# Measured VectorE durations in a kernel's own static schedule, and weight loads three groups later

## The chip, the cores and the metric

The kernel runs on one core of one Trainium2 chip. The metric is the device time of one execution in microseconds (us). Before the change the median was 1032.4 us (three runs, 1031.57 to 1032.62). The profile is one further execution of 1032.84 us, whose span from first to last instruction was 1031.0 us.

## The reference, cut to what matters

Linear attention produces 4608 tokens of width 512. A gate gives each token a score for each of eight experts, eight rounds of row and column normalisation turn the scores into a table P, and the output is the sum of eight two-layer experts, each weighted by its column of P.

```
x = attention(q, k, v, w_phi)            # 8 x 8 heads, 576 tokens, width 64 -> [4608, 512]
P = np.exp(x @ w_gate - max)             # [4608, 8]
for _ in range(8):                       # the "routing"
    P /= P.sum(1, keepdims=True) + 1e-09
    P /= P.sum(0, keepdims=True) + 1e-09
    P *= N / E
for e in range(8):
    out += P[:, e:e+1] * (np.maximum(x @ w1[e], 0) @ w2[e])
```

## The kernel before

The kernel orders its own instructions. Each operation is first recorded with an engine and an estimated duration; a list scheduler in the kernel then plays the whole program through with those estimates and so fixes one order per engine. On the chip every engine works through its list in order and waits where data is not there yet (in the routing's timeline below, a small matmul that waits 0.47 us holds up the large ones behind it). So a wrong estimate never breaks the result, but it places an operation too early or too late among its neighbours.

```
class Op:
    def after(self, user):                       # when a user of this operation may start
        if user.eng == self.eng and not self.nbytes:
            return self.stop + (0.0 if self.eng == "PE" else 0.04)
        return self.end
# ... cut ...
def dve(el, fn, r=(), w=(), shared=False):       # VectorE: el is an estimate in elements
    plan.op("DVE", el / 960.0 + 0.07, 0.15, fn, r, w, shared=shared)
```

The routing is a chain on VectorE. Each of its eight rounds ends in one small matmul (24 columns) that sums over partitions. Meanwhile TensorE has the matmuls of expert 0, so the small matmuls are put between those.

```
for it in range(8):
    # u = L * c_bc; rr = 1 / sum(u); wv = L * rr; cs = column sum of wv; two subtractions
    pe(24, ... mm(pc, colw, high(cs)) ...)       # the small matmul
    # c_bc = 1 / sum of the three parts in pc
```

Experts 1 to 7 each take nine groups of 512 tokens. They use sums of quarter matrices so that seven products do the work of eight. In expert 1 the sums of x ("X sums") are made by VectorE in buffers S, stored to DRAM, and read back by every expert as X. The sums of an expert's weights are made by VectorE from the freshly loaded w1 and w2.

```
ring("s_p", [128, 4, 256], BF16, "S", 5)         # five buffers S: X sums and hidden sums
# ... cut ...
for e in range(1, E):
    w1, w2 = load_w(e, ["late", ("acc", 2, 0, 0)] if e > 1 else ["late"])
    # ... cut: sums of weights, groups
```

The key `("acc", 2, 0, 0)` makes the load wait for the last write to that accumulator, which is group two of the preceding expert.

## Time and profile before

| stage (profile of before) | from, to (us) | TensorE |
|---|---|---|
| attention, with expert 0 begun | 0 to 204 | some 11 us idle, 10 of them in the first 60 us |
| routing beside expert 0 | 204 to 253 | small waits at seven small matmuls |
| experts 1 to 7 | 253 to 1020 | one gap, at 310 us, otherwise nearly full |
| last products and store | 1020 to 1031 | 4.5 us idle at the end |

The first lines are from the page: busy time and share of the span of each engine, and the chain of waits that ended last.

```profile
PE 1010.8 (98%) x9469; PEld 838.2 (81%) x9504; DVE 826.1 (80%) x1600; ACT 705.9 (68%) x1530; POOL 458.3 (44%) x480
...
PE 90%; DVE 4%; ACT 3%; DMA 2%; issue 1%; SPq 0%; DVEq 0%; ACTq 0%
```

TensorE (PE) bounds the kernel, so only its idle time can be won. The next lines are its timeline in the routing of the kernel before. The columns are the start, the length, engine, line, operation, output and inputs, sizes and number; in brackets stands the idle time before it and what ended it. Of the names, cs holds the column sums, hT the hidden values of an expert, and ps is an accumulator of TensorE.

```profile
211.15 1.89 PE L573 MATMUL ps<-xT,w 128*128 128x512 bf16 x8
213.35 0.17 PE L573 MATMUL ps<-cs,colw 128*128 128x24 bf16 x1 [0.31 <-DVE cs L1129]
213.37 1.89 PE L573 MATMUL ps<-w,hT 128*128 128x512 bf16 x8
...
217.03 0.17 PE L573 MATMUL ps<-cs,colw 128*128 128x24 bf16 x1 [0.47 <-DVE cs L1129]
```

The small matmul at 213.35 us waits for VectorE's last subtraction, and the eight large ones behind it wait too. The bracket understates the loss: ends of matmuls are modelled, and the eight before it were issued at 0.2155 us each, so the next could have started at 212.87 us. Seven small matmuls wait like this. The same chain on VectorE, one round of it, in the timeline of before:

```profile
221.61 0.20 DVE L1138 RECIPROCAL c_bc<-c_bc 128x8 f32<-128x8 f32 x1
221.84 0.46 DVE L1111 TENSOR_TENSOR T<-L,c_bc 128x288 f32<-128x288 f32 x1
222.34 0.45 DVE L1114 TENSOR_REDUCE rr<-T 128x36 f32<-128x288 f32 x1
222.82 0.38 DVE L1116 RECIPROCAL rr<-rr 128x36 f32<-128x36 f32 x1
223.24 0.46 DVE L1117 TENSOR_TENSOR T<-L,rr 128x288 f32<-128x288 f32 x1
223.73 0.68 DVE L1120 TENSOR_REDUCE cs<-T 128x8 f32<-128x288 f32 x1
224.44 0.37 DVE L1129 TENSOR_TENSOR cs<-cs 128x8 f32<-128x8 f32 x2
225.09 0.18 DVE L1135 TENSOR_REDUCE c_bc<-ps 128x8 f32<-128x24 f32 x1 [0.28 <-PE ps L573]
```

VectorE has no rest in the chain except for the matmul. The plan's estimate for the 288-element operations was 0.37 us; from the multiply at 221.84 to the reduce that needs it are 0.50 us.

The second place is expert 1, where expert 2's weights are loaded at 296.57 us. The chain of waits of before in this window (start, length, what):

```profile
298.14 8.75 DMA xd<-S
306.88 0.02 issue
306.91 2.43 DVE S L1181 x3
309.34 0.61 DVE hT L1305
309.95 0.04 issue
310.00 2.02 PE ps L1273 x17
```

A store of X sums takes 8.75 us, VectorE waits for the buffer that it reads, and TensorE waits for VectorE. The matmul before the gap was issued at about 308.55 us; at 0.109 us each the next was due at 308.66, so 1.34 us are lost.

### The profile page before, as it was taken

To read this page: it belongs to the slowest core of one execution; us is meant where nothing else is said; L and a number is where in the kernel's file an instruction comes from. 1 tells how busy PE (TensorE), PEld (TensorE's weight loads), DVE (VectorE), ACT (ScalarE), POOL (GpSimd) and SP (SyncE) were. 2 spreads that over 40 slices of the span, in tenths; PEclk is the share of its full clock that TensorE was granted. 3 is DMA by queue.
4 is the path that set the end of the run, shared out by engine and by line. 5 is a ranking of instruction groups with operands and counts; after the bars stand their busy time and mean duration, and the time that the engine had idled before them with its cause. 6 is when DMAs were issued, how large, how long until landed. Compare 5 with 4: busy or idle time off the path is not lost.

```text
span 1031.0 us, 24290 instructions
## 1 busy us (share of the span) xinstructions
PE 1010.8 (98%) x9469; PEld 838.2 (81%) x9504; DVE 826.1 (80%) x1600; ACT 705.9 (68%) x1530; POOL 458.3 (44%) x480
## 2 busy tenths in 40 slices
PE   7899999999999999999999999999999999999998
PEld 5666666635888888888888888888888888888886
DVE  7999989985889877778787877787787778777775
ACT  7999999834877766666665666666666666666663
POOL 5778764400344444444444434444444443344342
PEclk9999999999999999999999999999999999999999
DMA  9999977160263212511161116111431116114333
GB/s 254 178 192 190 179 131 124 35 150 1 97 139 114 63 42 57 108 42 52 43 129 47 42 43 123 42 52 37 85 88 50 42 43 123 42 42 126 131 124 123
DMA packets 112500, 96.03 MB, mean 93 GB/s; under 512 B 54144, under 2 KB 87040, under 8 KB 112384
## 3 DMA queue, kind: packets, MB, share of 16 engines
q1 hardware_dynamic: 80576, 70.55, 26.5%
q0 software_dynamic: 31648, 23.86, 16.3%
q8 instruction: 74, 1.21, 0.5%
q14 instruction: 42, 0.34, 0.1%
q10 hardware_dynamic: 160, 0.07, 0.0%
HBM read 94.98 MB, written 14.16 MB: 106 GB/s over the span
## 4 chain that ended last, share of the span: by engine, by line
PE 90%; DVE 4%; ACT 3%; DMA 2%; issue 1%; SPq 0%; DVEq 0%; ACTq 0%
PE ps L1273 72%; PE ps L573 15%; PE ps L856 2%; DMA xd<-S 1%; ACT q L569 1%; ACT k L569 1%; DMA acc<-in_k_dram 1%; DVE S L1181 0%; PE ps L703 0%; DVE cs L1120 0%; DVE m L565 0%; DVE wx L565 0%; DVE T L1111 0%; DVE T L1117 0%; DVE rr L1114 0%
## 5 line engine op out<-in xcount | busy, mean ns | idle before, releaser
L1428 POOL TENSOR_TENSOR acc<-acc,V 128x512 f32<-128x512 f32 x248 | 314.5, 1279 | 490.1 <-ACT V L1425 428.6
L1301 ACT COPY U<-ps 128x512 f32<-128x512 f32 x378 | 216.9, 587 | 169.9 <-PE ps L1273 157.5
L1305 DVE CUSTOM_DVE_ANT_0 hT<-ps,U 128x512 bf16<-128x512 f32 x378 | 254.3, 686 | 83.1 <-PE ps L1273 56.3
L1425 ACT ACTIVATE V<-ps,P 128x256 f32<-128x256 f32 x496 | 208.7, 475 | 88.1 <-PE ps L1273 81.4
L1413 DVE SCALAR_TENSOR_TENSOR acc<-ps,P,acc 128x256 f32<-128x256 f32 x372 | 158.6, 476 | 72.1 <-PE ps L1273 72.0
L1273 PEld LDWEIGHTS <-S 128*128 128x128 bf16 x1984 | 194.1, 98 | 22.6
L1273 PEld LDWEIGHTS <-T 128*128 128x128 bf16 x1512 | 147.9, 98 | 17.4 <-issue 0.3
L1273 PEld LDWEIGHTS <-hT 128*128 128x128 bf16 x1488 | 145.6, 98 | 16.9
L1273 PE MATMUL ps<-X,T 128*128 128x256 bf16 x1008 | 150.2, 273 | 0.0
L1273 PE MATMUL ps<-T,S 128*128 128x256 bf16 x1056 | 135.8, 273 | 0.0
L1273 PEld LDWEIGHTS <-wx 128*128 128x128 bf16 x1152 | 112.7, 98 | 14.9 <-issue 1.6
L1181 DVE TENSOR_TENSOR S<-hT 128x1024 bf16<-128x1024 bf16 x124 | 91.3, 742 | 9.9 <-ACT hT L1310 9.9
L1273 PEld LDWEIGHTS <-w 128*128 128x128 bf16 x864 | 84.5, 98 | 9.8
L1273 PE MATMUL ps<-xT,wx 128*128 128x256 bf16 x576 | 88.5, 273 | 1.2 <-DVE hT L1305 1.2
L1273 PE MATMUL ps<-X,wx 128*128 128x256 bf16 x576 | 86.8, 273 | 0.0
L1310 ACT ACTIVATE hT<-ps 128x512 bf16<-128x512 f32 x126 | 72.9, 608 | 7.8 <-PE ps L1273 7.8
L1273 PE MATMUL ps<-wx,hT 128*128 128x256 bf16 x560 | 77.3, 273 | 0.0
L1273 PE MATMUL ps<-xT,T 128*128 128x256 bf16 x504 | 76.4, 273 | 0.0
L573 PE MATMUL ps<-xT,w 128*128 128x512 bf16 x270 | 71.5, 379 | 0.7
L573 PE MATMUL ps<-w,hT 128*128 128x512 bf16 x276 | 69.7, 379 | 0.5
L1273 PE MATMUL ps<-T,hT 128*128 128x256 bf16 x496 | 68.5, 273 | 0.0
L1273 PE MATMUL ps<-xT,w 128*128 128x256 bf16 x432 | 66.8, 273 | 0.0
(129 smaller groups left out, 1425.9 us busy)
## 6 DMA issues: line engine op xcount, KB each, us to landing
X<-xd SPq DMA_DIRECT2D x126, 256.0 KB, 2.6
wx<-in_moe_w_dram POOLq DMA_DIRECT2D x8, 1024.0 KB, 12.6
v_m<-in_v_dram SPq DMA_DIRECT2D x15, 512.0 KB, 5.5
out_dram<-acc SPq DMA_DIRECT2D x14, 512.0 KB, 3.0
w<-in_moe_w_dram POOLq DMA_DIRECT2D x6, 1024.0 KB, 13.3
xd<-S SPq DMA_DIRECT2D x18, 256.0 KB, 3.8
qk<-in_k_dram POOLq DMA_DIRECT2D x12, 256.0 KB, 6.1
qk<-in_q_dram POOLq DMA_DIRECT2D x12, 256.0 KB, 6.5
```

The source lines that it names most:

```text
L569: act(el, lambda: nc.scalar.activation(out=dst(), in_=src(), func=ACT.Exp, bias=0.0, scale=scale), r, w)
L573: nc.tensor.matmul(out_, lhsT=lhsT, rhs=rhs, start=start, stop=stop)
L856: pe(65, lambda j=j: nc.tensor.matmul(pn()[:, j * D1:j * D1 + D1], lhsT=s["T"][x]()[:, j % 2, 2 * h + j // 2, :] if j < 4 else r["T"][x]() ...
L1181: lambda: f.tensor_tensor(out=out_(), in0=x(), in1=y(), op=op), r, w, **kw)
L1273: pe(256, lambda i=i, k=k, z=z: nc.tensor.matmul(bank()[:, 256 * i:256 * i + 256], lhsT=lhs(k, i), rhs=rhs(k), start=first and z, stop=k = ...
L1301: act(512, lambda: nc.scalar.copy(out=u[fp][n]().rearrange("p a b -> p (a b)"), in_=x[fp]()), [x[fp]], [u[fp][n]])
L1305: dve(515, lambda: nc.vector._custom_dve(ADD_SAT, out=out_(fp, i, j), in0=bank[fp]().rearrange("p (a b) -> p a b", a=2), in1=u[fp][n](), s ...
L1310: act(512, lambda: nc.scalar.activation(out=out_(fp, i, j), in_=x[fp]().rearrange("p (a b) -> p a b", a=2), func=ACT.Relu, bias=0.0, scale ...
L1413: dve(320, lambda n=n, ts=ts: nc.vector.scalar_tensor_tensor(out=acc[g][:, ts, 256 * j:256 * j + 256], in0=bank()[:, 256 * n:256 * n + 256 ...
L1425: act(370, lambda n=n: nc.scalar.activation(out=u()[:, n, :], in_=bank()[:, 256 * n:256 * n + 256], func=ACT.Copy, bias=0.0, scale=P[:, 4 ...
L1428: pool(695, lambda: nc.gpsimd.tensor_tensor(out=acc[g][:, 2 * i:2 * i + 2, 256 * j:256 * j + 256], in0=acc[g][:, 2 * i:2 * i + 2, 256 * j: ...
```

## The change

The intent is to let the plan hold the measured durations of the routing's VectorE operations, so that the small matmuls stand where the chain really reaches them, and to load each expert's weights later.

```
-dve(288, lambda ...   # 288-element multiplies and row sum, three places
+dve(366, lambda ...
-dve(225, lambda ...   # reciprocal of 36
+dve(291, lambda ...
-dve(480, lambda ...   # column sum
+dve(576, lambda ...
-dve(16, lambda ...    # the two subtractions
+dve(86, lambda ...
-dve(24, lambda ...    # sum of three parts
+dve(102, lambda ...
-dve(8, lambda ...     # reciprocal of 8
+dve(122, lambda ...
... the final multiply into P likewise 288 -> 366 ...
-        w1, w2 = load_w(e, ["late", ("acc", 2, 0, 0)] if e > 1 else ["late"])
+        w1, w2 = load_w(e, ["late", ("acc", 5, 0, 0)] if e > 1 else ["late"])
```

No operation is added or removed. In the new order 22, 19, 22, 22, 19, 22 and 22 matmuls lie from one small matmul to the next, against 18, 15, 18, 15, 18, 15 and 15.

More of the change, by code (lines that the diff above doesn't have):

```diff
@@ L1110, in u @@
                     return table(ub)
-                dve(288, lambda u=u, c=c_bc: nc.vector.tensor_tensor(
+                dve(366, lambda u=u, c=c_bc: nc.vector.tensor_tensor(
                     out=u(), in0=L, in1=c()[:, None, :].to_broadcast([128, NT, E]),
                     op=ALU.mult), lk + [c_bc], uk, shared=True)
-            dve(288, lambda u=u, rr=rr: nc.vector.tensor_reduce(
+            dve(366, lambda u=u, rr=rr: nc.vector.tensor_reduce(
                 out=rr(), in_=u(), axis=AX.X, op=ALU.add), uk + ["late"], [rr])
-            dve(225, lambda rr=rr: nc.vector.reciprocal(out=rr(), in_=rr()), [], [rr])
-            dve(288, lambda rr=rr, wv=wv: nc.vector.tensor_tensor(
+            dve(291, lambda rr=rr: nc.vector.reciprocal(out=rr(), in_=rr()), [], [rr])
+            dve(366, lambda rr=rr, wv=wv: nc.vector.tensor_tensor(
                 out=table(wv), in0=L, in1=rr()[:, :, None].to_broadcast([128, NT, E]),
                 op=ALU.mult), lk + [rr], [wv], shared=True)
-            dve(480, lambda wv=wv, cs=cs: nc.vector.tensor_reduce(
+            dve(576, lambda wv=wv, cs=cs: nc.vector.tensor_reduce(
                 out=cs()[:, 0], in_=table(wv).transpose([0, 2, 1]), axis=AX.X, op=ALU.add), [wv], [cs])
@@ L1128, in routing @@
             for i in range(2):
-                dve(16, lambda i=i, cs=cs, high=high: nc.vector.tensor_tensor(
+                dve(86, lambda i=i, cs=cs, high=high: nc.vector.tensor_tensor(
                     out=cs()[:, i + 1], in0=cs()[:, i], in1=high()[:, E * i:E * i + E],
@@ L1134, in routing @@
             c_bc = new("c_bc")
-            dve(24, lambda pc=pc, c=c_bc: nc.vector.tensor_reduce(
+            dve(102, lambda pc=pc, c=c_bc: nc.vector.tensor_reduce(
                 out=c(), in_=pc()[:, 0:3 * E].rearrange("p (a b) -> p b a", a=3), axis=AX.X,
                 op=ALU.add), [pc], [c_bc])
-            dve(8, lambda c=c_bc: nc.vector.reciprocal(out=c(), in_=c()), [], [c_bc])
-        dve(288, lambda c=c_bc, wv=wv: nc.vector.scalar_tensor_tensor(
+            dve(122, lambda c=c_bc: nc.vector.reciprocal(out=c(), in_=c()), [], [c_bc])
+        dve(366, lambda c=c_bc, wv=wv: nc.vector.scalar_tensor_tensor(
             out=P, in0=table(wv), scalar=float(N) / float(E),
```

## The prediction

> **What bounds the kernel now.** TensorE: 98% busy on the page, 90% of the chain of waits. From 310 us on it is never idle: the windows show 917 or 918 matmuls per 100 us, one 128x256 matmul every 0.109 us, until the last group. Its 20 us of idle time: the first 60 us (10 us, not touched), the routing (210 to 240 us: 3 us in the windows), one gap at 308.7 to 310.0 us, and the last 5 us (not touched).
>
> **Routing.** Eight iterations each run a VectorE chain and then one small matmul, which the plan puts between expert 0's matmuls. TensorE works in order: where the plan thinks the chain too short, the small matmul stands too early and everything behind it waits. Plan against trace: 0.37 and 0.457 us for the 288-element operations, 0.57 and 0.676 for the column sum, 0.087 and 0.167 for the subtractions, 0.078 and 0.203 for the last reciprocal. The measured period is 3.70 us without an accumulator copy on VectorE, 4.15 with one. In the old order a small matmul comes 15 or 18 matmuls after the last; the 14 or 17 large ones, at 0.2155 us, take 3.0 or 3.7 us: 0.5 to 0.6 us too little, and the timeline shows seven waits. From the first small matmul (209.18 us) to expert 1's first (253.26 us) stand 185 large and 8 small ones: about 40.1 us of work in 44.1 us. About 4.0 us are lost.
>
> The changed order has 22 or 19 between small ones, 19 only where no copy falls inside: 4.5 or 3.9 us, over 4.15 or 3.70. All seven waits should go. The routing itself ends later (last small matmul near 240.1 us instead of 236.4, table P near 241.5 instead of 237.8); the weight sums that expert 1's first matmul needs follow, done near 245, and TensorE arrives near 249.2.
>
> **Weight load.** Expert 2's load is issued at 296.6 us, amid the stores of the X sums. One store (298.14 us) then takes 8.75 us instead of about 2; VectorE waits for its buffer (306.91 us), and TensorE loses about 1.4 us. The Trainium skill (Trainium Kernel Development and Optimization, Key Constraints) says that all DMA queues share the same 16 engines; this trace agrees. In the new order the load comes behind the last of these stores, so the gap should go. Later experts' loads merely move three groups (36 us); w1 lands some 8 us after issue, and its four sums still stand about one group before the next expert's first matmul. The eight sums (5 us) now fall in two groups, where VectorE goes from 9.4 to about 11 us busy of 12.2. Main risk: stalls of 0 to 0.5 us at each of six transitions.
>
> **Prediction.** 4.0 + 1.4 us off, 0.3 given back: 1027.3 us, 8 in 10 between 1025.6 and 1029.4. Faster by over 2%: 0.01; within 2%: 0.98; slower: 0.01.
>
> **What would show it.** Right: no TensorE waits on the subtractions at L1129 between 209 and 242 us; expert 1's first matmul near 249.2 us; no gap in expert 1; 110 us per expert; the same tail. Wrong: expert 1 waits for its weight sums; VectorE waits for a weights DMA, and TensorE for VectorE at expert changes; an X store still slow near 330 us.
>
> **What would make it wrong.** Weights landing after their planned sums; VectorE saturating in groups seven and eight.

## The result

The changed kernel takes 1026.85 us (median of six runs, 1026.29 to 1028.55), the kernel before 1032.47 us (six runs). The ratio is 0.9949, with a 95% interval from 0.9937 to 0.9962. Ratios in this document are the mean time of one kernel's fast runs over that of the other's of the same rounds, so they are not quite the ratio of the medians quoted.

The profile after has a span of 1026.8 us; that execution was the slowest of the six and began 1.3 us late (the matmuls of its last gate begin at 204.8 instead of 203.6 us, in a part the change does not touch). The busy times of the engines in the same windows, before and after (window, length, then busy time of PE, PEld, DVE, ACT, POOL with counts, granted clock, DMA share, GB/s). Before:

```profile
200.00:260.00 60.00, 56.91 (x337) 29.01 (x338) 44.02 (x116) 24.90 (x45) 1.74 (x2) 1.00 0.34 76
300.00:312.00 12.00, 10.83 (x100) 9.49 (x98) 11.26 (x19) 8.50 (x18) 5.58 (x4) 1.00 1.14 227
```

After:

```profile
200.00:260.00 60.00, 59.58 (x380) 32.37 (x385) 47.91 (x124) 27.35 (x50) 1.74 (x2) 1.00 0.35 80
300.00:312.00 12.00, 12.00 (x112) 10.75 (x111) 8.92 (x19) 9.54 (x21) 6.16 (x5) 1.00 0.21 68
```

TensorE is nearly full in the first window and full in the second, and the DMA traffic of the second has gone elsewhere. TensorE's timeline after, in the routing:

```profile
214.07 1.46 PE L573 MATMUL ps<-w,hT 128*128 128x512 bf16 x6
215.37 0.18 PE L573 MATMUL ps<-cs,colw 128*128 128x24 bf16 x1
215.40 0.59 PE L573 MATMUL ps<-w,hT 128*128 128x512 bf16 x2
...
219.28 0.18 PE L573 MATMUL ps<-cs,colw 128*128 128x24 bf16 x1
```

No bracket is left: 214.07 plus six times 0.2155 is 215.36, and the small matmul starts at 215.37. It is VectorE that now waits for the small matmul, as its timeline after shows:

```profile
228.63 0.18 DVE L1135 TENSOR_REDUCE c_bc<-ps 128x8 f32<-128x24 f32 x1 [0.67 <-PE ps L573]
...
232.54 0.18 DVE L1135 TENSOR_REDUCE c_bc<-ps 128x8 f32<-128x24 f32 x1 [0.50 <-PE ps L573]
```

The store queue and the load after, from the timelines of the SP and the POOL engine (start and length of issue):

```profile
327.85 0.99 SPq L1257 DMA_DIRECT2D xd<-S  x2
...
331.57 1.69 POOL L468 DMA_DIRECT2D w<-in_moe_w_dram  x2
```

The first of the last two stores is issued 3.7 us before the load, and both have landed when the load is issued. The chain of waits after, which has no wait left in the rest of expert 1:

```profile
255.66 2.25 DMA xd<-S
258.68 756.68 PE ps L1273 x6928
```

From 258.68 us on the chain is TensorE alone until the last products. Just before stands a gap of 0.23 us, which the kernel before has too.

For the experiments two lengths are read from TensorE's timeline, since they are free of the start's noise. "Routing" runs from the last gate's 32 small matmuls to expert 1's first matmul; it repeats to 0.01 us between kernels with the same order. "Experts" runs from there to the first recorded matmul of the last product; a few records are missing in a trace, so it is good to about 0.4 us. Part of that can be told: in five traces (before, experiments 1, 3 and 4, and the second run of group four) the first record of the last product is missing, so their experts lengths are 0.22 us too long.

| kernel | routing | experts | median (us) | before beside it | ratio, 95% interval |
|---|---|---|---|---|---|
| before | 49.70 | 766.41 | 1032.47 | | |
| changed | 45.68 | 764.69 | 1026.85 | 1032.47 | 0.9949, 0.9937 to 0.9962 |
| durations alone | 45.68 | 766.18 | 1028.28 | 1032.43 | 0.9958, 0.9946 to 0.9971 |
| load alone | 49.70 | 764.91 | 1030.68 | 1032.43 | 0.9984, 0.9972 to 0.9997 |
| load of expert 2 alone | 49.70 | 765.06 | 1030.70 | 1032.43 | 0.9988, 0.9974 to 1.0001 |
| before, six S | 49.70 | 765.80 | 1032.59 | 1032.43 | 0.9997, 0.9984 to 1.0009 |
| durations x 1.3 | 45.68 | 767.29 | 1029.55 | 1033.17 | 0.9958, 0.9943 to 0.9972 |
| dependent end, everywhere | 46.21 | 764.96 | 1031.94 | 1033.17 | 0.9996, 0.9973 to 1.0018 |
| small entries alone | 46.53 | 769.13 | 1029.55 | 1033.17 | 0.9956, 0.9940 to 0.9973 |
| load after group six | 45.68 | 772.61 | 1035.59 | 1033.17 | 1.0015, 1.0000 to 1.0030 |
| dependent end, routing alone | 45.89 | 765.25 | 1027.86 | 1033.55 | 0.9946, 0.9934 to 0.9958 |
| load after group four | 45.68 | 764.96 | 1027.01 | 1033.55 | 0.9939, 0.9928 to 0.9951 |
| load after group four, again | 45.67 | 765.18 | 1027.37 | 1032.09 | 0.9953, 0.9940 to 0.9967 |
| durations, six S, group two | 45.68 | 765.34 | 1028.23 | 1033.55 | 0.9952, 0.9939 to 0.9965 |

The runs came on four chips. On two of them the kernel before scattered (1031.75 to 1037.12, and 1031.98 to 1035.69 us), so the ratios of those rounds are the less exact; there the stage lengths decide.

### The profile page after: what moved, and what is told of

The parts are those of the page before. It is cut to its first block, busy times and chain, and to the rows that moved or that the text cites. A ratio compares the mean times of both kernels' runs of the same rounds, so it can differ in the third digit from the quotient of the medians.

```text
span 1026.8 us, 24281 instructions
## 1 busy us (share of the span) xinstructions
PE 1008.1 (98%) x9469; PEld 837.9 (82%) x9504; DVE 823.5 (80%) x1600; ACT 703.9 (69%) x1530; POOL 458.5 (45%) x480
## 4 chain that ended last, share of the span: by engine, by line
PE 93%; ACT 2%; DVE 1%; DMA 1%; SPq 1%; issue 1%; POOL 0%; DVEq 0%; ACTq 0%
PE ps L1273 74%; PE ps L573 17%; PE ps L856 2%; DMA acc<-in_q_dram 1%; ACT q L569 1%; ACT k L569 0%; SPq L495 0%; ACT wx L569 0%; SPq L551 0%; PE ps L885 0%; DMA xd<-S 0%; DVE ps L864 0%; DVE hT L1305 0%; DVE m L565 0%; POOL wx L761 0%
## 5 line engine op out<-in xcount | busy, mean ns | idle before, releaser
L1273 PE MATMUL ps<-X,T 128*128 128x256 bf16 x1008 | 152.4, 273 | 0.0
L1181 DVE TENSOR_TENSOR S<-hT 128x1024 bf16<-128x1024 bf16 x124 | 87.2, 712 | 10.1 <-ACT hT L1310 9.9
```

The costliest lines, as they stand in the source:

```text
L1181: lambda: f.tensor_tensor(out=out_(), in0=x(), in1=y(), op=op), r, w, **kw)
L1273: pe(256, lambda i=i, k=k, z=z: nc.tensor.matmul(bank()[:, 256 * i:256 * i + 256], lhsT=lhs(k, i), rhs=rhs(k), start=first and z, stop=k = ...
```

## The experiments

**1. The durations alone.** The load stays after group two.

```
 (changed kernel)
-load_w(e, ["late", ("acc", 5, 0, 0)] ...
+load_w(e, ["late", ("acc", 2, 0, 0)] ...
```

> The durations alone, weight load still after group two. My theory (two independent gains): the seven waits at the small matmuls of the routing go (4.0 us), the gap of TensorE in expert 1 (1.2 us in the timeline, behind an X-sum store of 8 to 9 us) stays. Time about 1028.4 us, ratio 0.9961. Rival (the new order as a whole removes the gap, and the load is idle): gap gone too, about 1027 us, ratio 0.9948.

The median is 1028.28 us. The routing is as short as in the changed kernel, with no wait at a small matmul. In expert 1 a store takes 8.36 us and TensorE has gaps:

```profile
294.59 8.36 DMA xd<-S
...
302.98 0.40 DVE S L1181
303.38 6.46 DMA xd<-S
```

VectorE waits twice for such stores (0.26 and 0.88 us), and TensorE twice for VectorE (0.54 and 0.19 us in the brackets of the timeline). The durations give the routing's 4.0 us and nothing else.

**2. The load alone.** Old durations.

```
 (kernel before)
-("acc", 2, 0, 0)
+("acc", 5, 0, 0)
```

> The load alone, old durations. Theory: all seven waits at the small matmuls stay as they were (0.3 to 0.5 us each), the gap in expert 1 is gone, the last X-sum store lands in about 2 us. Time about 1031.1 us, ratio 0.9987. Rival (load is idle or its later place costs at the expert changes): ratio 1.000 or above, gap still there or new gaps of TensorE at the starts of experts 2 to 7.

The median is 1030.68 us, 1.75 below the kernel before. All seven waits are there (0.29 to 0.48 us), and expert 1 has no gap; the stores take about 2 us. The two parts give 4.15 and 1.75 us by medians of the same rounds, together 5.9; the whole change gave 5.6. They add up, within the scatter.

**3. The load of expert 2 alone.**

```
 (kernel before)
-("acc", 2, 0, 0)
+("acc", 5 if e == 2 else 2, 0, 0)
```

> Old durations; only expert 2's load waits for group five, those of experts 3 to 7 stay after group two. Theory: the whole effect of the load lies in expert 1, where X sums are still being stored; so the same as the load alone, ratio 0.9987, gap gone, and no difference in experts 2 to 6. Rival (spreading or crowding of the weight sums matters in every expert): only about a sixth of the load's effect, or a different one.

The median is 1030.70 us, the same as with all loads moved, and the experts stage agrees within 0.15 us. The interval just reaches 1, so the time alone would not settle it; the timeline does: no gap in expert 1. For experts 3 to 7 it makes no difference whether the load stands after group two or five.

**4. Six buffers S instead of five.**

```
 (kernel before)
-ring("s_p", [128, 4, 256], BF16, "S", 5)
+ring("s_p", [128, 4, 256], BF16, "S", 6)
```

> The kernel before with six buffers S instead of five, loads after group two. Theory (TensorE's gap comes because VectorE waits for a buffer S that the slow store still reads): the store that overlaps the load still takes 8 to 9 us, but VectorE no longer waits for it and the gap of 1.2 us goes or shrinks below 0.3; ratio 0.9987. Rival (the gap comes from the slowed X load or from the shared port, not from the buffer): gap stays, ratio 1.000.

The time is a miss: 1032.59 us, ratio 0.9997. The two stores that overlap the load still take 7.4 and 8.1 us, and behind them VectorE waits for none and TensorE has no gap, as expected. But the new order has another gap, 5 us before the load is even issued:

```profile
292.47 1.03 PE L1273 MATMUL ps<-T,S 128*128 128x256 bf16 x8 [0.71 <-DVE acc L1413]
```

In VectorE's timeline of this kernel a subtraction that otherwise takes 0.42 us takes 1.50 just before:

```profile
289.54 1.50 DVE L1181 TENSOR_TENSOR S<-xT,S 128x512 bf16<-128x512 bf16 x1
```

Such long operations stand in the kernel before, too. There the wait for the store pushed a subtraction to 307.59 us, just behind the start of GpSimd's addition at 307.50. The timelines of VectorE and of GpSimd (POOL) in the kernel before:

```profile
306.91 0.42 DVE L1181 TENSOR_TENSOR S<-xT 128x512 bf16<-128x512 bf16 x1 [0.64 <-DMA xd<-S]
307.25 0.42 DVE L1181 TENSOR_TENSOR S<-xT,S 128x512 bf16<-128x512 bf16 x1
307.59 1.75 DVE L1181 TENSOR_TENSOR S<-hT 128x1024 bf16<-128x1024 bf16 x1
```

```profile
307.50 2.96 POOL L1428 TENSOR_TENSOR acc<-acc,V 128x512 f32<-128x512 f32 x2 [1.82 <-ACT V L1425]
```

The subtraction of 1024 elements takes 0.68 us elsewhere. The Trainium skill (SBUF — State Buffer, Who interferes with whom) says that a VectorE instruction with two SBUF inputs contends with a GpSimd instruction that reads SBUF, and that the shared port pair behind this is an exclusive lock. This trace agrees: the subtraction, whose inputs both lie in SBUF, began 0.09 us after the first of the two additions, lasted 1.07 us longer than alone and ended 0.54 us after that addition did. So the wait of 0.64 us cost more than itself: it moved VectorE into GpSimd's way, and the two delays together, 1.71 us with some slack, make TensorE's 1.34 us. No run here takes the shared port away by itself, so how the loss splits between the two was only read from the timeline.

**5. The durations 1.3 times too long.**

```
 (changed kernel; each routing entry as a duration x 1.3)
-dve(366, ...   dve(291, ...   dve(576, ...   dve(86, ...   dve(102, ...   dve(122, ...
+dve(496, ...   dve(398, ...   dve(769, ...   dve(132, ...  dve(153, ...   dve(179, ...
```

> The changed kernel, with every duration of the routing's VectorE operations 1.3 times the measured one. The order then puts 26 or 23 matmuls between small ones. My theory (an over-long plan costs nothing in the routing, as TensorE never waits, but delays table P and the weight sums of expert 1): routing stage as long as in the changed kernel (45.7 us from the last gate to expert 1's first matmul), VectorE waits about 1.3 us per iteration, and TensorE waits 0.3 to 2 us at the start of expert 1. Ratio to before 0.995 to 0.9965. Rival (only exact figures help; too long is as bad as too short): about 4 us lost again, ratio 0.998 or above.

The median is 1029.55 us. The routing is 45.68 us, and VectorE waits 0.85 to 1.53 us for seven of the eight small matmuls. But P is finished at 248.2 us, just when TensorE reaches expert 1 at 248.27, and TensorE then waits:

```profile
253.70 0.49 PE L1273 MATMUL ps<-X,wx 128*128 128x256 bf16 x3 [1.77 <-DVE hT L1305]
```

The experts stage is 2.6 us longer than in the changed kernel; I had expected 0.3 to 2 us. In this run too long an estimate cost nothing in the routing and was paid once, behind it; too short an estimate is paid in every round. How the cost grows with still longer estimates was not measured.

**6. The end of a dependent operation, in the whole plan.** In the kernel before, one operation of the routing followed by an unrelated one shows a shorter spacing than the chain does. VectorE's timeline of before, at the routing's start:

```profile
205.19 0.44 DVE L1114 TENSOR_REDUCE rr<-L 128x36 f32<-128x288 f32 x1
205.55 0.41 DVE L1181 TENSOR_TENSOR S<-xT,S 128x512 bf16<-128x512 bf16 x1
```

The reduce and the unrelated subtraction start 0.36 us apart, which is the plan's old 0.37; in the chain above the reduce and the reciprocal that needs it start 0.48 us apart. The Trainium skill (VectorE: DVE Perf Modes, The DRAIN you can't avoid) says that after a VectorE operation the next one starts once the pipeline is empty, and that one which is not held starts earlier. By held the page means an operation whose operands start in other groups of partitions than those before; that the need for a result delays an operation too is read from this trace alone: the unrelated subtraction starts 0.08 us before the reduce's recorded end, and the dependent reciprocal about 0.03 us after it. The column sum shows the same: 0.71 us to the subtraction that needs it (at 223.73 us above), 0.58 us to an unrelated operation at the routing's start, where the plan's old figure was 0.57. So the old entries were about right for neighbours that do not depend on each other. This experiment keeps them and lengthens only the step to a dependent operation, for all of VectorE.

```
 (kernel before, load after group five)
-            return self.stop + (0.0 if self.eng == "PE" else 0.04)
+            return self.stop + {"PE": 0.0, "DVE": 0.12}.get(self.eng, 0.04)
```

> The load after group five, the old durations, but in the plan a VectorE operation that needs the one before it may start 0.12 us instead of 0.04 us after its end. My theory (the old figures fit operations issued back to back; what they miss is the uncovered end of an operation that the next depends on): the order puts 21 or 18 matmuls between small ones, waits of at most 0.05 us are left at two or three of them, routing stage 45.7 to 46.1 us; ratio about 0.995, like the changed kernel. It also alters the order of the attention stage before 200 us, where I expect no more than 1 us either way. Rival (the durations themselves are what matters): waits of 0.3 us remain.

In the routing there is no wait in a bracket. Its 46.21 us lie just above what was expected, and they hold two large matmuls (0.43 us) more than the routing of the other kernels, so for equal work it is 45.78 us. But the time, 1031.94 us, is a miss. The new rule also changed the order of the attention stage; in the profile, which fell in one of the two longest of the six runs (1037.75 and 1035.76 us), the last gate comes at 213.2 us instead of 203.6, and one wait alone is 4.09 us:

```profile
PE ps L573 <- ACT q L569: 4.5, 3, 4.1
```

(Columns of the waits view: who waited for whom, us in total, times, longest.) Why the attention's order is worse with this rule was not looked into and stays open. In its four quicker runs this kernel took 1031.3 to 1032.0 us, some 4 us more than experiment 9 has with the attention's order left alone.

**7. The small entries alone.**

```
 (kernel before)
-dve(16, ...   dve(24, ...   dve(8, ...
+dve(86, ...   dve(102, ...  dve(122, ...
```

> The kernel before with only the three small entries corrected (16 to 86, 24 to 102, 8 to 122): 0.35 of the 0.76 us that an iteration was short. The order has 20 or 17 matmuls between small ones, 4.1 and 3.5 us. Theory (the loss is the difference of chain and spacing, iteration by iteration): waits of 0 to 0.25 us, 0.6 to 1.3 us lost in all instead of 4.0; routing stage 46.3 to 47.0 us; ratio about 0.997. Rival (it takes the large entries): waits as before, ratio 1.000.

The routing is 46.53 us, within what was expected: 3.17 of the 4.02 us for 0.35 of the 0.76 us by which a round was short. The gain is not proportional; this fits a loss that is only what the spacing lacks, in matmuls that come in whole numbers. The profiled run (1033.02 us, the slowest of six) still has the gap of the early load, and it is larger, 2.60 us, with a store of 9.1 us. The other five runs are 2.9 to 4.3 us quicker, so this gap probably varies from run to run. Not all of this run's 769.13 us is the gap: for 3.4 us behind it the granted clock was 0.5 and a matmul came every 0.213 us, which is another 1.6 us. Experiment 6 has the same 3.4 us at 0.5 behind its wait of 4.09 us; behind experiment 5's wait of 1.77 us the clock stayed at 1.0.

**8. The load after group six.**

```
 (changed kernel)
-("acc", 5, 0, 0)
+("acc", 6, 0, 0)
```

> The changed kernel with the load after group six, 12 us later. w1 then lands about 3 us before the next expert's first matmul, and three of its sums have to run in between. Theory (a later load is free until the first sums miss the first matmul): at the margin, 0 to 1 us lost at each of six experts; ratio 0.995 to 1.001. Rival (crowding of all eight sums into few groups already costs): over 1 us per expert.

The median is 1035.59 us; this is slower than the changed kernel by over 8 us. TensorE's timeline has one large gap at each of the six changes of expert, nearly equal:

```profile
356.57 1.03 PE L1273 MATMUL ps<-wx,hT 128*128 128x256 bf16 x8 [0.99 <-ACT V L1425]
...
468.37 1.03 PE L1273 MATMUL ps<-w,hT 128*128 128x256 bf16 x8 [0.99 <-ACT V L1425]
```

The experts stage is 7.9 us longer than in the changed kernel, 1.3 us at each change; I had expected 0 to 1. In VectorE's timeline the sums of w1 now begin at 355.86 us, when TensorE has already begun with expert 2 (353.67 us), although w1 landed at 350.07 us:

```profile
355.86 0.69 DVE L1181 TENSOR_TENSOR T<-w 128x1024 bf16<-128x1024 bf16 x1
```

With the load after group five the first of them runs at 344.71 us, before the change of expert. The bracket of the gap names ScalarE (ACT), which reads the product just before. In the changed kernel matmuls of expert 2, some of them on such a sum, stand between these two products (357.44 to 358.31 us), here they come later, and TensorE goes straight to the second one and waits. This link is read from the two timelines and was not tested by itself. Of the places tried, group five is the last that is free; the next group costs.

**9. The dependent end, in the routing alone.** Like experiment 6, but the step is 0.12 us only for the routing's operations, so that the attention stage keeps its order.

```
 (kernel before, load after group five)
-            return self.stop + (0.0 if self.eng == "PE" else 0.04)
+            return self.stop + (0.0 if self.eng == "PE" else self.gap)
...
+    n0 = len(plan.ops)
     routing()
+    for o in plan.ops[n0:]:
+        o.gap = 0.12          # 0.04 for all others
```

> Load after group five, old durations; only inside the routing may an operation that needs the one before it start 0.12 us instead of 0.04 us after its end; the attention stage keeps its old order. The order has 21, 20 or 18 matmuls between small ones. Theory (the uncovered end of a dependent operation is what the plan missed): routing stage 45.7 to 46.3 us, no wait of 0.15 us or more at a small matmul, no gap in expert 1, ratio 0.994 to 0.996, as the changed kernel. If it is slower than the changed kernel by over 1 us, the theory of the dependent end is not enough.

The median is 1027.86 us, the routing 45.89 us, the ratio 0.9946; no small matmul waits 0.15 us or more. With the old durations and one constant the plan recovers all but 0.2 us of what the measured durations recover. It is within about 1 us of the changed kernel, not better.

**10. The load after group four, twice.**

```
 (changed kernel)
-("acc", 5, 0, 0)
+("acc", 4, 0, 0)
```

> The changed kernel with the load after group four. The load of expert 2 is then issued about when an X-sum store of the next group goes out, as it was with group two. Theory (what counts is whether a store overlaps the load): one store takes over 6 us, VectorE waits for a buffer S, TensorE loses 1 to 2.6 us in expert 1; experts stage 765.7 to 767.5 us against 764.7; ratio 0.9955 to 0.9975. Rival (any later place than group two is as good): no gap, 764.7 us, ratio 0.9945.

This is a miss, against my theory in its simple form. The load is issued at 316.80 us and a store goes out at 318.37, in the midst of it, but there is no gap, and 1027.01 us is the changed kernel's time. The landing view of that store (engine, count, size, us from issue to landing) in this kernel:

```profile
xd<-S SPq DMA_DIRECT2D x1, 256.0 KB, 7.4
```

and of the corresponding one in the kernel before:

```profile
xd<-S SPq DMA_DIRECT2D x1, 256.0 KB, 8.7
```

In the kernel before, VectorE could have used the buffer at about 306.27 us, 8.13 us after the issue; the store was 0.6 us late. Here VectorE asks at 326.42 us, 8.05 us after the issue; the store was 0.6 us early. Overlap alone therefore costs nothing; what counts is whether the store lands before VectorE returns to the buffer. A second run was to tell whether 7.4 us was chance.

> The kernel with the load after group four once more, for a second profile. In the first, the overlapping store took 7.4 us and VectorE asked for its buffer 8.1 us after the store was issued; with the load after group two three profiles have 8.4 to 9.1 us. First theory (the length of an overlapping store varies from run to run, and only over some 8.1 us does it cost anything): this store may come out above 8.1 us and then shows a wait of VectorE and a gap of TensorE. Second theory (after group four the store is quicker for a reason of its place): 7.2 to 7.8 us again, no gap, median about 1027.0 us.

The second store took 7.1 us, VectorE did not wait, and the median was 1027.37 us. With the load after group two all three profiles with five buffers have 8.4 to 9.1 us; with the load after group four both have 7.1 and 7.4. In all five the store is issued 1.6 us after the load. So it does not look like chance, and why the same store beside the same kind of load is 1 to 2 us quicker two groups later stays open. Experiment 6's profile holds one more such case: in its order the load after group five overlaps the last store of X sums, which takes 7.84 us, and again VectorE does not wait and TensorE has no gap.

**11. The durations with six buffers S, load after group two.** A second draw of experiment 4.

```
 (changed kernel)
-("acc", 5, 0, 0)          ring("s_p", [128, 4, 256], BF16, "S", 5)
+("acc", 2, 0, 0)          ring("s_p", [128, 4, 256], BF16, "S", 6)
```

> The durations, six buffers S, load still after group two: a second draw of the buffer test, in the new order. Theory (the gap needs the wait for a buffer): the store still takes 6 to 9 us, VectorE waits for none, TensorE has no gap behind it; experts stage 764.7 to 765.6 us, ratio 0.9945 to 0.9955. A gap from a VectorE operation held up while GpSimd works may still come, as in the first draw.

The two stores behind the load take 7.0 and 7.7 us, VectorE waits for none, and TensorE has no gap behind them. As in the first draw there is a gap of 0.71 us before the load, after a subtraction of 1.49 us beside a GpSimd addition. The experts stage is 765.34 us, the median 1028.23 us. So a sixth buffer does remove this gap without moving the load, at the price of an order that happens to have another; moving the load removes it without that price.

No run beats the changed kernel clearly; the load after group four equals it.

## Why the prediction was right

**The sum.** Predicted were 4.0 us from the routing, 1.4 us from the gap, 0.3 us given back: 1027.3 us. Measured were 1026.85 us. The routing gave 49.70 - 45.68 = 4.02 us. The gap of expert 1 was 1.34 us at the matmul pitch; with the missing record taken off, the experts stage is 0.9 to 1.5 us shorter in the kernels that have no gap in expert 1, 1.5 us in the changed kernel. Nothing was given back: in the changed kernel the largest gap of TensorE between expert 1's start and the last product is the 0.23 us at 258.45 us, which stands in the kernel before as well.

**The waits at the small matmuls.** All seven are gone, and VectorE waits instead, 0.50 to 0.73 us in seven of the eight rounds, which costs nothing. Experiment 1 shows that the durations do this alone. Experiment 9 and the spacings in experiment 6 put it more sharply than the prediction did: the old durations fit unrelated neighbours, and what was missing is the end of an operation that a dependent neighbour has to wait for. In the chain itself nearly every operation depends on the one before, so there the two wordings come to the same.

**The routing ends later, and that fits.** P was predicted near 241.5 us and is finished at 242.6, in a profile that began 1.3 us late; expert 1's first matmul is at 250.51 us, predicted 249.2, with the same shift. Experiment 5 shows the margin: with P finished 7.8 us later, counted from the last gate, 2.6 us are lost.

**The load.** The gap is gone and the place is right: experiment 3 has the whole effect from expert 2's load alone. But the step "the load comes behind the last of these stores, so the gap should go" was too simple as a cause. Experiment 10 overlaps load and store and has no gap. The cause is narrower: with the load after group two the store lands after VectorE needs its buffer again, and the delay runs into GpSimd's addition.

**Crowding of the weight sums.** VectorE was predicted to go to about 11 us busy of 12.2 in the last groups of an expert. The windows after, for the last two groups of expert 2:

```profile
442.20:454.40 12.20, 12.20 (x114) 10.94 (x112) 9.27 (x18) 7.63 (x17) 5.38 (x5) 1.00 1.09 188
454.40:466.60 12.20, 12.20 (x114) 10.93 (x112) 10.97 (x21) 7.57 (x17) 5.04 (x4) 1.00 0.28 73
```

The third number with a count is VectorE: 9.27 and 10.97 us, so the 11 us come in one of the groups, and TensorE stays full. The eight weight sums were more spread than predicted: five fall in these windows, from 450.69 us on, and three behind them, up to 469.60 us. The feared 0 to 0.5 us per change of expert did not come, but the margin is one group: experiment 8 loses 1.3 us per change.

## What to carry to other kernels

In a statically ordered kernel, read what each planned wait costs on the bounding engine from the timeline, and compare the plan's estimate with the start-to-start spacing in a dependent chain, not with that of independent neighbours. Err on the long side for a side chain whose result is wanted later: here too short was paid in every round, and 1.3 times too long once, at the end. When a load hurts, look for the small transfer beside it whose buffer someone wants back soon: here moving the load and one more buffer both cured that (the buffer with another gap in its order), and the load could be moved only as far as its first consumer allowed.

## What the Trainium skill lacked or had wrong

- VectorE: DVE Perf Modes (The DRAIN you can't avoid) has a size for the flush, but none for how much later an operation starts that needs the result of the one before than one that does not. Here a 288-element fp32 row sum and an unrelated operation start 0.36 us apart, the row sum and the operation that needs it 0.48 us apart.
- Trainium Kernel Development and Optimization (Key Constraints) says that queues on the same DMA engines interleave. Its text has no size for the effect; here a store of 256 KB takes 2.0 us alone and 7.1 to 9.1 us when it is issued 1.6 us after a 2 x 1024 KB weight load, and the spread by the load's place is unexplained.
